# Bucket attention and a rational FFN on one core: token pieces loaded into the buffers of their parts, and operands, values and weights loaded at other steps

## The chip, the cores and the metric

The kernel runs on one core of a Trainium2 chip. A core has a matrix engine (TensorE, PE in the profile; its weight loads are PEld), a vector engine (VectorE, DVE), a scalar engine (ScalarE, ACT), a general one (GpSimd, POOL) and SyncE (SP), whose queue issues nearly all DMA transfers here. The metric is device time in microseconds (us) of one execution; lower is better.

## The reference

Two stages. Attention over 4 batches x 8 heads, 768 positions, head size 64, where a query sees only the keys of its own hash bucket; then a feed-forward network (FFN) with a rational function, over 3072 tokens of 512 values.

```python
q_bits = (einsum('bhsd,dk->bhsk', q, proj) > 0);  k_bits likewise
mask = bucket(q_bits)[:, :, :, None] == bucket(k_bits)[:, :, None, :]
scores = where(mask, q @ k.T / 8, -1e9);  scores -= scores.max(-1)
attn = exp(scores);  attn /= attn.sum(-1) + 1e-9
x = (attn @ v) rearranged to 3072 x 512
h = x @ w_in                                   # 512 x 2048
g = (a0 + a1*h + a2*h**2 + a3*h**3) / (1 + |b0|*|h| + |b1|*h**2 + 1e-6)
out = g @ w_out                                # 2048 x 512
```

`w_in` and `w_out` arrive as 64-bit floats; everything else and the output have 32 bits.

## The kernel before

Matrix products are made exact enough by splitting an operand into a rounded high part and the low part that is left, so that a product takes several passes.

**Attention** goes over 16 pairs of heads. For a pair `p`: `load(p)` brings the raw operands q and k into one of two buffers of the tag "raw" (`qkf` in the profile); `high` (ACT) and `low` (DVE) split them, `high_move`, `second_low` and `second_high` move parts between halves of the partitions (SP: `q<-q`, `k<-k`, `q<-lo`, `k<-lo`); `bits`, `penalties` and `maskrows` write mask rows (`q<-mb`, `k<-mb`); `maxstep` finds row maxima (`m<-psm`), which `shift_turn` and `shift_rows` put in as a row (`q<-mt`). Then twelve steps of `scores` (`pss`), each followed by exponentials on ACT (`E<-pss`) and sums of them (`acc`); `load_v` brings the values, and `values` multiplies them in two blocks of six steps (`psv<-E,v`); `values_out` copies the result (`col`, `xo`) and `values_store` stores it to memory (`x_d<-xo`). `sums` and `sums_store` do the same for the denominators (`psu`, `sr`, `s_d`), and `recips` turns the denominators of a batch into reciprocals in memory (`r_d`).

**Weights.** Beside attention, `weights(i)` prepares both weight matrices in 32 portions. An even `i` loads a portion of w_in (`wr<-w_in`), an odd one of w_out (`wr<-w_out`); two buffers `wr` serve both. ACT and DVE convert the portion from 64 bits in several steps (`ws<-wr`, `wr<-wr`, `ws<-ws,wr`) and split it; w_in stays on chip as `wi_hi` and `wi_lo`, w_out is stored to `wo_d` and comes back in the FFN.

**FFN.** Six blocks of 512 tokens. `Tokens.load(t, c)` brings a block in three pieces: values from `x_d`, reciprocals from `r_d` spread over 64 partitions, a product of both on DVE, a rounding copy on ACT into the high part `xh`, a subtraction on DVE into the low part `xl`. The parts of an even block lie in the two "raw" buffers; the last piece lies in two small ones. Per block 16 steps: `Gemm1` (`psh`), the rational function on ACT and DVE, the second product (`pso`). The first block's pieces are loaded while attention ends.

**Order.** The order of all work up to the FFN is written out by hand: `at(p, s, f, ...)` puts a call at place 12p+s, `spread` puts the parts of a generator (each up to its `yield`) at several places, and the calls are issued by rising place. Each engine and SP's queue keep that order. The numbers stand in the tables `MID`, `FIRST` (pairs 0 and 1) and `LAST` (the end). Some that matter here:

- `load(p)` at 12(p-4) + `MID["load"]` for p > 3; `load_v(p)` at 12(p-1) + `MID["load_v"]` for p > 1;
- the parts of `weights(i)` at 12(i // 2) + `MID["weights"][i % 2]`, for i < 2 those of `FIRST`;
- the parts of piece c of the first block at 180 + `LAST["tokens"][c]`: load, product, copy, subtraction;
- `coefficients` loads the FFN's coefficients (`ab<-coef`) at 12 and reads them on ACT (`absb`) at 14.

A DMA that fills a buffer which is still in use waits on SP, and what stands behind it on SP waits too.

Of the kernel before, what the change touches and what calls it, by code (L numbers as in the profile page):

```python
# [7 lines left out]
F32 = mybir.dt.float32  # L8
# [5 lines left out]
ALU = mybir.AluOpType  # L14
# [4 lines left out]
P = 128  # L19
S = 768  # L20
# [10 lines left out]
NCC = DM // P  # L31
NFC = DFF // P
NTK = 512
# [8 lines left out]
    group=6, values=[0.66, 0.05], values_out=3.5, maxima=7.17,  # L42
    maxima_steps=[0, 1.15, 1.73, 2.64, 3.32, 5.08, 5.86, 6.98, 8.0, 8.84, 10.26, 11.37], sums=14.65, sums_store=17.37,
    high=[-0.41, 1.19], low=[1.06, 3.35], bits=2.81, penalties=4.05, high_move=1.9, maskrows=5.61, second_low=-2.2,
    second_high=2.69, load_v=10.99, shift_turn=8.61, shift_rows=8.82, load=9.0, recips=[20.0, 22.0, 23.0],
    weights=[[1.44, 4.0, 4.1, 5.09, 5.49, 7.11, 9.5, 9.75, 17.5], [8.05, 10, 10.65, 11.5, 12.38, 14.29, 16.34, 19.32, 21.22]],
    weights_last=[0.5, 0.8, 1.0, 1.2],
)

# [1 line left out]
    maxima1=4.62, rate1=0.45, maxima2=9.5, rate2=0.82, high=[3.25, 3.53], low=[6.0, 7.3], bits=7.15, penalties=7.25,  # L51
    high_move=4.53, maskrows=8.2, second_low=4.25, second_high=4.35, load_v=4.78, group=2,
    values=[2.35, 2.65, 2.32, 2.35, 0.35, 0.61], values_out=3.02, high1=[-0.27, -5.58], low1=[11.24, 4.95],
    high_move1=20.05, load2=21.89, load3=3.8, penalties1=-6.57, maskrows1=3.69,
    weights=[[-5.7, 6.64, 6.7, 11.42, 12.19, 18.75, 21.75, 38.77, 44.13], [8.03, 9.04, 9.24, 11.12, 14.81, 15.27, 15.99, 17.91, 46.81]],
    warm=6, warms=[3, 3, 3, 1, 1, 1], maxima00=[-4.26, -2.29, -4.17, 1.67, -1.15, 2.77], shift00=[2.15, 4.99],
    shift0=[3.67, 3.44], ahead=3, scores=[[3.68, 3.82, 7.26], [6.03, 8.25, 12.4]], pen01=[4.77, 14.55], comp01=3.35,
# [3 lines left out]

LAST = dict(
    group=6, values=[0.28, 0.44], values_out=1.39, vout14=3.03,
    tokens=[[-7.43, -5.11, -2.83, -1.09], [-0.04, 3.83, 4.5, 5.2], [6.0, 9.38, 9.45, 9.53]], terms=7.05, ffn=[13.61, 16.09, 16.14],
    sums=16.96, wide=8, share=11, third=0, sums14=14.69, sumst14=22.46,
)
TINY = 2.0 ** -80
# [105 lines left out]
def attention(ctx, tc, nc, raw, ps_b, tail, tokens, early, operands_to_terms, ffn, load, QF, KF, v, w_in, w_out, wo_d, ident, cst, ones, prj,  # L173
# [302 lines left out]
    def at(p, s, f, *args):  # L476
        plan.setdefault(12 * p + s, []).append((f, args))
# [5 lines left out]
    for p in range(NPAIR):  # L483
        mid = 0 < p < NPAIR - 1
        n = MID["group"] if mid else (FIRST if p == 0 else LAST)["group"]
        for s in range(12):
            if p > 0 or s >= FIRST["ahead"]:
                at(p, s, scores, p, s)

            if p > 1:  # L490
                at(p - 2, MID["maxima"] + MID["maxima_steps"][s] if p > 2 else FIRST["maxima2"] + FIRST["rate2"] * s, maxstep, p, s)
            if s % n == n - 1:
                for i in range(s - n + 1, s + 1):
                    at(p, s + (MID["values"][s // n] if mid else (FIRST if p == 0 else LAST)["values"][s // n]), values, p, i)
            if s % NT == NT - 1:
                at(p, s + (LAST["vout14"] if (p, s) == (NPAIR - 2, 11) else MID["values_out"] if mid else (FIRST if p == 0 else LAST)["values_out"]), values_out, p, s // NT)
        for hf in range(2):
            at(p, 6 * hf + 9, values_store, p, hf)
        if p < NPAIR - 1:
            at(p, MID["sums"] if p < NPAIR - 2 else LAST["sums14"], sums, p)  # L500
            at(p, MID["sums_store"] if p < NPAIR - 2 else LAST["sumst14"], sums_store, p)
        if p > 1:
            for t in range(2):
                at(p - 2, (MID if p > 2 else FIRST)["high"][t], high, p, t)
                at(p - 2, (MID if p > 2 else FIRST)["low"][t], low, p, t, nc.vector if p > 2 else nc.gpsimd)
            if p % 2 == 0:
                at(p - 2, (MID if p > 2 else FIRST)["bits"], bits, p)
                at(p - 2, (MID if p > 2 else FIRST)["penalties"], penalties, p)
            at(p - 2, (MID if p > 2 else FIRST)["high_move"], high_move, p)
            at(p - 2, (MID if p > 2 else FIRST)["maskrows"], maskrows, p)  # L510
        if p > 0:
            at(p - 1, (MID if p > 1 else FIRST)["second_low"], second_low, p)
            at(p - 1, (MID if p > 1 else FIRST)["second_high"], second_high, p)
            at(p - 1, (MID if p > 1 else FIRST)["load_v"], load_v, p)
        if p > 1:
            at(p - 1, MID["shift_turn"], shift_turn, p)
            at(p - 1, MID["shift_rows"], shift_rows, p)
        if p > 3:
            at(p - 4, MID["load"], load, p)
        if p % NHP == NHP - 1 and p + 1 < NPAIR:  # L520
            spread(p, MID["recips"], recips(p // NHP))
    for i in range(2 * NFC):
        o = 12 * (i // 2)
        w = list(FIRST["weights"][i]) if i < 2 else list(MID["weights"][i % 2])
# [92 lines left out]
class Tokens:  # L617
# [214 lines left out]
```

## Time and profile before

| | before |
|---|---|
| median of 3 runs | 937.54 us (936.46 to 938.1) |
| the profiled execution, time | 937.44 us |
| its span, first to last instruction | 935.6 us |
| mean granted TensorE clock | 0.997 |
| busy share: PE, DVE, ACT, POOL | 99%, 90%, 69%, 47% |
| chain that ended last, by engine | PE 91%, DVE 3%, DMA 3%, ACT 2% |
| DMA moved | 111.57 MB, mean 119 GB/s |

The page gives busy times, a picture of the span in 40 slices, DMA queues, the chain of work that ended last, and the costliest groups of instructions. Attention with the weights takes the first 406 us or so, and the FFN the rest. In both, PE is busy nearly always. A row of the timeline has the start and the duration in us, the engine, the operation with its output and inputs, and in square brackets how long the engine was idle before it and what released it. SPq is the queue on which SP issues DMAs; the duration there is that of the issue, not of the transfer. All helper calls share line 93, so work is told apart by its tiles.

### The profile page before, as it was taken

The page shows a single profiled execution, that of the slowest core. Times are in us where ns is not written, and L with a number is a line of the kernel's source. Part 1 is how long each engine was busy: PE and PEld are TensorE (multiplying, and loading weights), DVE is VectorE, ACT ScalarE, POOL GpSimd, SP SyncE. Part 2 cuts the span into 40 slices and gives each one's busy share as a digit, 9 for nine tenths or more (in the row PEclk, how much of TensorE's full clock was granted, in tenths as well). Part 3 has the DMA queues.
Part 4 walks back from the last instruction along what each step waited for, and adds up shares of the span by engine and source line. Part 5 has one row for each costly group of instructions (what it writes and reads, how often), then busy time and mean ns, then how long its engine had stood idle before and what let it go on. Part 6 is the DMA issues. An engine that isn't in the chain of part 4 may idle for free.

```text
span 935.6 us, 13659 instructions
## 1 busy us (share of the span) xinstructions
PE 922.6 (99%) x4678; PEld 701.4 (75%) x4678; DVE 840.5 (90%) x1029; ACT 648.5 (69%) x1229; POOL 436.6 (47%) x362
## 2 busy tenths in 40 slices
PE   8999999999999999899999999999999999999997
PEld 4666666666767677568888888888888888888886
DVE  6799889878988898688998999899999999998996
ACT  7577767667767676777767776776676677677664
POOL 5587878777878787522222223223222222222222
PEclk9999999999999999999999999999999999999999
DMA  6768878778877778346412100210021002001001
GB/s 196 214 179 225 231 219 230 220 208 226 240 217 224 226 195 216 132 133 226 143 28 75 38 23 1 79 35 23 1 80 41 17 34 79 23 1 46 0 1 46
DMA packets 51243, 111.57 MB, mean 119 GB/s; under 512 B 9347, under 2 KB 20215, under 8 KB 51173
## 3 DMA queue, kind: packets, MB, share of 16 engines
q1 hardware_dynamic: 50740, 110.47, 40.3%
q8 instruction: 37, 0.61, 0.3%
q14 instruction: 34, 0.27, 0.1%
q10 hardware_dynamic: 432, 0.23, 0.1%
HBM read 56.82 MB, written 21.17 MB: 83 GB/s over the span
## 4 chain that ended last, share of the span: by engine, by line
PE 91%; DVE 3%; DMA 3%; ACT 2%; SPq 1%; issue 1%; ACTq 0%; DVEq 0%
PE psh L93 28%; PE pso L93 28%; PE pss L93 13%; PE psv L93 12%; PE psm L93 7%; PE psu L93 2%; DMA wr<-w_in 2%; DVE m L93 2%; PE psb L93 1%; SPq L93 1%; ACT E L93 1%; DMA r<-r_d 0%; DMA qkf<-kT 0%; DVE ws L93 0%; DVE wr L93 0%
## 5 line engine op out<-in xcount | busy, mean ns | idle before, releaser
L93 POOL TENSOR_TENSOR gl<-c,gh 128x512 fp32r<-128x512 f32 x96 | 134.6, 1402 | 387.6 <-ACT gh L93 378.3
L93 ACT ACTIVATE E<-pss 128x384 f32<-128x384 f32 x384 | 167.8, 493 | 106.1 <-PE pss L93 92.1
L93 PE MATMUL pso<-wo,gh 128*128 128x512 f32 x768 | 235.4, 389 | 0.0
L93 DVE TENSOR_REDUCE m<-psm 128x1 f32<-128x768 f32 x192 | 179.7, 949 | 34.7 <-PE psm L93 31.2
L93 POOL TENSOR_TENSOR acc<-E,E 128x384 f32<-128x384 f32 x124 | 154.4, 1263 | 87.7 <-ACT E L93 87.5
L93 PE MATMUL pss<-q,k 128*128 128x384 f32 (+2 forms) x768 | 171.9, 349 | 0.4 <-ACT col L93 0.4
L93 PEld LDWEIGHTS pso<-wo,gh 128*128 128x128 f32 x768 | 144.1, 188 | 29.8
L93 PEld LDWEIGHTS pss<-q,k 128*128 128x128 f32 (+2 forms) x768 | 136.2, 191 | 28.4 <-issue 17.0
L93 PE MATMUL psh<-xh,wi_hi 128*128 128x512 f32 x384 | 149.6, 390 | 0.0
L93 PE MATMUL psh<-xl,wi_hi 128*128 128x512 f32 x384 | 149.4, 389 | 0.0
L93 PE MATMUL psh<-xh,wi_lo 128*128 128x512 f32 x384 | 149.4, 389 | 0.0
L93 PE MATMUL pso<-wo,gl 128*128 128x512 f32 x384 | 148.4, 389 | 0.0
L93 ACT ACTIVATE h<-psh 128x512 f32<-128x512 f32 x96 | 57.4, 598 | 130.7 <-PE psh L93 130.6
L93 POOL TENSOR_TENSOR acc<-acc,E 128x384 f32<-128x384 f32 x123 | 137.3, 1135 | 11.1 <-ACT E L93 10.9
L93 PE MATMUL psv<-E,v 128*64 128x385 f32 x768 | 134.3, 492 | 4.0 <-ACT E L93 3.5
L93 DVE SCALAR_TENSOR_TENSOR c<-c,ab,r 128x512 f32<-128x512 f32 x96 | 135.6, 1413 | 0.0
L93 PEld LDWEIGHTS psv<-E,v 128*64 128x64 f32 x768 | 52.6, 136 | 71.4 <-issue 61.8
L93 PE MATMUL psm<-k,q 76*128 76x384 f32 (+1 forms) x384 | 102.2, 348 | 1.8 <-DVE m L93 1.0
L93 DVE SCALAR_TENSOR_TENSOR w<-h,absb,w 128x512 f32<-128x512 f32 x96 | 74.0, 771 | 15.4 <-ACT w L93 15.2
L93 PEld LDWEIGHTS psh<-xh,wi_hi 128*128 128x128 f32 x384 | 72.0, 187 | 16.1 <-issue 1.2
L93 PEld LDWEIGHTS pso<-wo,gl 128*128 128x128 f32 x384 | 72.1, 188 | 15.1
L93 PEld LDWEIGHTS psh<-xl,wi_hi 128*128 128x128 f32 x384 | 72.1, 188 | 14.9
(78 smaller groups left out, 1218.3 us busy)
## 6 DMA issues: line engine op xcount, KB each, us to landing
q<-q SPq DMA_DIRECT2D x45, 192.0 KB
k<-k SPq DMA_DIRECT2D x45, 192.0 KB
wr<-w_in SPq DMA_DIRECT2D x16, 512.0 KB
wr<-w_out SPq DMA_DIRECT2D x16, 512.0 KB
wo_d<-wr SPq DMA_DIRECT2D x16, 512.0 KB
wo<-wo_d SPq DMA_DIRECT2D x16, 512.0 KB
qkf<-qT SPq DMA_DIRECT2D x16, 384.0 KB
qkf<-kT SPq DMA_DIRECT2D x16, 384.0 KB
```

What stands on the lines that cost most here:

```text
L93: return self.tc.keep_in_program_order(issue(*args, **kwargs))
```

## The change

Two things. First, `Tokens.load` no longer loads values and reciprocals into the buffers "lo0" and "lo1": it loads the values into the place of the low part and the reciprocals into the place of the high part, multiplies both into a new tile `y` ("lo0" for pieces 0 and 2, "lo1" for piece 1), rounds `y` into the high part and subtracts into the low part. The number of instructions and of bytes stays the same. The parts' tiles are taken when the load is issued, not after the product.

Second, places in the order change: raw operands from 9.0 to 5.7 (pair 4 keeps 9.0), values from 10.99 to 8.9, the load of each w_in portion but the first from 1.44 to -1.0, and most parts of the token pieces.

```diff
-    second_high=2.69, load_v=10.99, shift_turn=8.61, shift_rows=8.82, load=9.0, recips=[20.0, 22.0, 23.0],
-    weights=[[1.44, 4.0, 4.1, 5.09, 5.49, 7.11, 9.5, 9.75, 17.5], [8.05, ...]],
+    second_high=2.69, load_v=8.9, shift_turn=8.61, shift_rows=8.82, load=5.7, recips=[20.0, 22.0, 23.0],
+    weights=[[-1.0, 4.0, 4.1, 5.09, 5.49, 7.11, 9.5, 9.75, 17.5], [8.05, ...]],
...
-    high_move1=20.05, load2=21.89, load3=3.8, penalties1=-6.57, maskrows1=3.69,
+    high_move1=20.05, load2=21.89, load3=3.8, load4=9.0, penalties1=-6.57, maskrows1=3.69,
...
-    tokens=[[-7.43, -5.11, -2.83, -1.09], [-0.04, 3.83, 4.5, 5.2], [6.0, 9.38, 9.45, 9.53]], terms=7.05, ...
+    tokens=[[-8.9, -5.11, -2.83, -1.09], [-2.9, 1.5, 2.2, 3.83], [7.1, 10.4, 10.5, 10.6]], terms=7.05, ...
...
-            at(p - 4, MID["load"], load, p)
+            at(p - 4, MID["load"] if p > 4 else FIRST["load4"], load, p)
...
     def load(self, t, c):
-        nc, raw = self.nc, self.raw
-        w = min(S, NCC * NTK - c * S)
-        x = raw.tile([P, w], F32, tag="lo0", name=f"x{t}_{c}", bufs=1)
-        r = raw.tile([P, w], F32, tag="lo1", name=f"r{t}_{c}", bufs=1)
+        nc = self.nc
+        hi, lo = self.place(t, c, "h"), self.place(t, c, "l")
+        w = hi.shape[1]
+        x, r = lo.bitcast(F32), hi.bitcast(F32)
...
         yield
-        nc.vector.tensor_tensor(out=x, in0=x, in1=r, op=ALU.mult)
-        yield
-        hi, lo = self.place(t, c, "h"), self.place(t, c, "l")
-        nc.scalar.copy(hi, x)
-        yield
-        nc.vector.tensor_tensor(out=lo, in0=x, in1=hi.bitcast(F32), op=ALU.subtract)
+        y = self.raw.tile([P, w], F32, tag=f"lo{c % 2}", name=f"y{t}_{c}", bufs=1)
+        nc.vector.tensor_tensor(out=y, in0=x, in1=r, op=ALU.mult)
+        yield
+        nc.scalar.copy(hi, y)
+        yield
+        nc.vector.tensor_tensor(out=lo, in0=y, in1=hi.bitcast(F32), op=ALU.subtract)
```

More of the change, by code (lines that the diff above doesn't have):

```diff
@@ L44 @@
     high=[-0.41, 1.19], low=[1.06, 3.35], bits=2.81, penalties=4.05, high_move=1.9, maskrows=5.61, second_low=-2.2,
-    second_high=2.69, load_v=10.99, shift_turn=8.61, shift_rows=8.82, load=9.0, recips=[20.0, 22.0, 23.0],
-    weights=[[1.44, 4.0, 4.1, 5.09, 5.49, 7.11, 9.5, 9.75, 17.5], [8.05, 10, 10.65, 11.5, 12.38, 14.29, 16.34, 19.32, 21.22]],
+    second_high=2.69, load_v=8.9, shift_turn=8.61, shift_rows=8.82, load=5.7, recips=[20.0, 22.0, 23.0],
+    weights=[[-1.0, 4.0, 4.1, 5.09, 5.49, 7.11, 9.5, 9.75, 17.5], [8.05, 10, 10.65, 11.5, 12.38, 14.29, 16.34, 19.32, 21.22]],
     weights_last=[0.5, 0.8, 1.0, 1.2],
@@ L63 @@
     group=6, values=[0.28, 0.44], values_out=1.39, vout14=3.03,
-    tokens=[[-7.43, -5.11, -2.83, -1.09], [-0.04, 3.83, 4.5, 5.2], [6.0, 9.38, 9.45, 9.53]], terms=7.05, ffn=[13.61, 16.09, 16.14],
+    tokens=[[-8.9, -5.11, -2.83, -1.09], [-2.9, 1.5, 2.2, 3.83], [7.1, 10.4, 10.5, 10.6]], terms=7.05, ffn=[13.61, 16.09, 16.14],
     sums=16.96, wide=8, share=11, third=0, sums14=14.69, sumst14=22.46,
```

## The prediction, made before the changed kernel ran

> **What bounds the kernel now.** I read the head of the page first: the span, and how much of it TensorE (PE) works.
>
> ```profile
> span 935.6 us, 13659 instructions
> ...
> PE 922.6 (99%) x4678; PEld 701.4 (75%) x4678; DVE 840.5 (90%) x1029; ACT 648.5 (69%) x1229; POOL 436.6 (47%) x362
> ```
>
> PE is idle for 935.6 - 922.6 = 13.0 us in all, and apart from a lowered clock that is all that a change of loads can win. The run that was profiled took 937.44 us, 1.84 us more than its span, and the median of the runs shown is 937.54 us; I reckon against 937.44. About 0.2% of it, 1.9 us, is what a measurement of this kernel can tell from no change.
>
> Next the timeline around the passage from the last attention pair (15) to the FFN, where the page's slices show PE below full share. I write "step 12p+s" for a place in the written plan: step s of pair p.
>
> ```profile
> 376.36 0.37 SPq L93 DMA_DIRECT2D v<-v  x1
> ...
> 381.59 0.32 SPq L93 DMA_DIRECT2D x<-x_d  x1
> ...
> 384.45 0.58 ACT L93 ACTIVATE xo<-psv,col 128x384 f32<-128x384 f32 x1
> ...
> 384.79 1.36 DVE L93 TENSOR_TENSOR acc<-E,E 128x384 f32<-128x384 f32 x1
> 384.90 0.58 SPq L93 DMA_DIRECT2D wr<-w_in  x1
> ...
> 389.23 0.96 DVE L93 TENSOR_TENSOR x<-x,r 128x768 f32<-128x768 f32 x1 [2.41 <-DMA r<-r_d]
> ...
> 390.20 0.67 ACT L93 ACTIVATE ws<-wr 128x512 f32<-128x512 f32 x1 [2.74 <-DMA wr<-w_in]
> ...
> 392.61 1.24 PE L93 MATMUL psv<-E,v 128*64 128x385 f32 x4 [2.15 <-ACT E L93]
> ...
> 395.66 0.32 SPq L93 DMA_DIRECT2D x<-x_d  x1
> ...
> 401.76 0.62 ACT L93 CAST xh<-x 128x512 fp32r<-128x512 f32 x1 [2.45 <-DVE x L93]
> ...
> 404.70 1.25 PE L93 MATMUL psv<-E,v 128*64 128x385 f32 x4 [0.63 <-ACT E L93]
> ...
> 405.87 0.50 PE L93 MATMUL psh<-xh,wi_hi 128*128 128x512 f32 x1
> ```
>
> Read it by releasers. ScalarE (ACT) stands still 2.74 us before 390.20 for `wr<-w_in`; the last exponential of the first half of pair 15 is queued behind that, and PE waits 2.15 us for it before 392.61. ACT stands still again 2.45 us before 401.76, for the third token piece's product on VectorE (DVE), whose load was issued at 395.66. FFN products start at 405.87. The waits of the SP queue and of the engines say why the two loads were late:
>
> ```profile
> SPq L93 <- DVE xl L93: 133.2, 12, 17.0
> ```
>
> ```profile
> ACT ws L93 <- DMA wr<-w_in: 7.3, 4, 3.5
> ```
>
> SP held token pieces until `xl` of the piece before was written, because both pieces used the same two buffers; the weight load stood behind the second piece (381.59, then 384.90). The wait for `wr<-w_in` came four times, 7.3 us in total, so there is one more large one. The chain shows what it cost:
>
> ```profile
> 129.66 4.03 PE psv L93 x24
> ...
> 177.28 4.03 PE psv L93 x24
> ...
> 226.38 4.03 PE psv L93 x24
> ```
>
> ```profile
> 192.26 0.59 SPq L93 DMA_DIRECT2D v<-v  x1
> 192.89 0.49 SPq L93 DMA_DIRECT2D wr<-w_in  x1
> ```
>
> ```profile
> 203.07 0.69 ACT L93 ACTIVATE ws<-wr 128x512 f32<-128x512 f32 x1 [3.50 <-DMA wr<-w_in]
> ```
>
> Value blocks of the same place lie two pairs apart: 177.28 - 129.66 = 47.62 us, then 226.38 - 177.28 = 49.10. The second is 1.5 us too long, and it holds the 3.50 us ACT wait for the load issued at 192.89, with the values issued just before at 192.26.
>
> **The change part by part.** *Token pieces (t = 0).* The number of instructions stays; only a buffer `y` for the product is new, alternating between two, and nothing in SP's order waits for `xl` any more. Piece 2 moves from step 179.96 to 177.10, ahead of the first weight load of the next group, which moves from 181.44 to 179.00. SP is free after the values' load (376.36), so piece 2 goes out at about 376.8. In the old run the same six issues took 384.90 - 381.59 = 3.3 us, so `wr<-w_in` goes out at about 380.1, 4.8 us earlier, and its 2.74 us wait goes. What is late next: the product of piece 2 now stands at step 181.5 on DVE and its rounding copy at 182.2 on ACT, directly behind the copy `xo`, which ends at 384.45 + 0.58 = 385.03. DVE is busy with the sum `acc` until 384.79 + 1.36 = 386.15, and the product takes 0.96 (row 389.23), so ACT now waits from 385.03 to 387.11, 2.1 us, ahead of three exponentials. Net gain there: 2.74 - 2.08 = 0.66 us.
>
> *Piece 3* moves from step 186.0 to 187.10 but loses its wait. SP can issue it once the store of `xo` has gone (about 385.6, estimated from 385.03) instead of at 395.66, so the data are there some 10 us earlier. Its ACT copy now stands at 190.5, behind the exponential of step 190, not ahead of it, so the 2.45 us wait no longer holds that. But the last load of w_out (step 188.05) and its conversion now stand ahead of the copy, and the product still follows DVE's sums. I let half of the 2.45 us come back as those waits and take 1.2 us; the ends are 0 and 2.45. The passage then gives 0.66 + 1.2 = 1.9 us, and psh starts near 404.0.
>
> *The clock.* The same passage was also slow in another way:
>
> ```profile
> 394.00:395.00 1.00, 1.00 (x5) 1.00 (x5) 1.00 (x3) 0.49 (x1) 0.00 (x0) 0.65 0.05 16
> 395.00:396.00 1.00, 1.00 (x5) 1.00 (x4) 1.00 (x2) 0.91 (x3) 0.00 (x0) 0.50 0.00 0
> 396.00:397.00 1.00, 1.00 (x4) 1.00 (x4) 0.19 (x1) 0.81 (x3) 0.03 (x1) 0.50 0.36 49
> 397.00:398.00 1.00, 1.00 (x5) 1.00 (x5) 0.70 (x1) 1.00 (x3) 0.98 (x1) 0.64 0.86 291
> ```
>
> The granted clock in the last column but two was 0.65, 0.50, 0.50 and 0.64 in four slices of 1 us, 1.7 us lost, right after the 2.15 us gap. My new gap is about 0.7 us shorter. [...] I credit nothing here: ACT, not PE, set most of that stretch. The ends are 0 and 1.7 us of gain.
>
> *Raw operands, values, weights in the middle pairs.* In each pair SP's order was: mask rows, `wo_d` store, `w_out`, shift rows, `x_d` store, raw operands (2 x 384 KB), low parts (4 x 192 KB), values, `w_in`. It becomes: mask rows, raw operands, `wo_d`, `w_out`, shift rows, values, `x_d`, low parts, `w_in`. Values go out right after the shift rows, past seven transfers, and `w_in` has 0.79 MB less ahead of it. For a price of 0.79 MB I take this row:
>
> ```profile
> 120.00:144.00 24.00, 24.00 (x153) 16.64 (x153) 21.22 (x25) 17.13 (x38) 18.85 (x17) 1.00 0.78 218
> ```
>
> 218 GB/s at a DMA share of 0.78 is 279 GB/s when busy, so 0.79 MB takes 2.8 us. The stall of 3.50 us thus shrinks to below 1 us, and of its 1.5 us I take 1.2 as won. In the other middle pairs PE is busy 24.00 of 24 us, as here, so an earlier load wins nothing.
>
> What this pays for is `w_out`, which now stands behind the raw operands in 11 pairs (1 to 11):
>
> ```profile
> 109.73 0.45 SPq L93 DMA_DIRECT2D wo_d<-wr  x1
> ...
> 115.65 0.67 ACT L93 ACTIVATE ws<-wr 128x512 f32<-128x512 f32 x1
> ...
> 116.14 4.10 PE L93 MATMUL psv<-E,v 128*64 128x385 f32 x24
> ...
> 116.78 0.87 ACT L93 ACTIVATE E<-pss 128x384 f32<-128x384 f32 x2
> ```
>
> ```profile
> 207.74 0.45 SPq L93 DMA_DIRECT2D wo_d<-wr  x1
> ```
>
> ```profile
> 212.74 0.68 ACT L93 ACTIVATE ws<-wr 128x512 f32<-128x512 f32 x1 [0.33 <-DMA wr<-w_out]
> ```
>
> The raw operands go out where `wo_d` did, so `w_out` lands 2.8 us later. In the worst pair it was there 212.74 - 207.74 = 5.0 us after `wo_d` was issued (ACT waited 0.33); in the usual pair ACT comes for it 115.65 - 109.73 = 5.92 us after. With the same landing ACT now waits 5.0 + 2.8 - 5.92 = 1.9 us in a usual pair. Behind it stands the exponential of step 11: its first half ends at 116.78 + 0.87 / 2 = 117.2, and PE reads it after 20 of 24 value products, at 116.14 + 4.10 x 20 / 24 = 119.6. So 2.3 us are free, and 1.9 are covered. Where ACT comes early, as at 212.74, the wait is 2.8 us and 0.5 are lost; that pair was early only because of the stall before it. I take 0.2 us lost; the ends are 0 and 5.5 us (0.5 in each of 11). The shift rows also stand behind this: the queue ahead of them is done 5.0 + 2.8 = 7.8 us after `wo_d` used to be issued, and the scores that need them follow the value block, which ends at 116.14 + 4.10 = 120.2, 10.5 us after it: covered.
>
> *First pair.* `w_in` number 2 moves from 13.44 to 11.00, ahead of the coefficients at 12.00, but its buffer comes free only where it did, since it uses that of number 0.
>
> ```profile
> 48.53 0.59 SPq L93 DMA_DIRECT2D ab<-coef  x1
> 50.47 0.33 SPq L93 DMA_DIRECT2D wr<-w_in  x1
> ```
>
> ```profile
> 52.08 0.22 ACT L93 ACTIVATE absb<-ab 128x1 f32<-128x1 f32 x1
> ...
> 53.58 0.48 ACT L93 COPY sr<-psu 128x384 f32<-128x384 f32 x1 [0.61 <-PE psu L93]
> ...
> 54.88 0.62 ACT L93 CAST wr<-ws 128x512 fp32r<-128x512 f32 x1
> ```
>
> ```profile
> 56.51 1.50 DVE L93 TENSOR_TENSOR wr<-ws,wr 128x512 fp32r<-128x512 f32 x1
> ```
>
> ```profile
> 384.90 5.28 DMA wr<-w_in
> ```
>
> So the coefficients go out after 50.47 instead of at 48.53, behind 512 KB. The only row with the time of such a load is the last, 5.28 us with token pieces ahead of it; with an emptier queue I estimate 4.1, so 54.6 at the earliest and 55.8 with 5.28. ACT comes for them at 52.08 and waits 2.5 us; 0.61 was idle anyway (row 53.58), so the cast of 54.88 ends near 57.4 instead of 55.50, and DVE's subtraction starts 0.9 us after its 56.51. DVE is on the chain here. I take +0.9; the ends are 0 (the small transfer passes the large one) and +2.1. [...]
>
> *The rest.* In the FFN only buffers change; PE runs without a gap, and token loads there lose a wait of SP that nobody waits for: 0.
>
> Sum: -1.9 (passage) - 1.2 (stall at 203) + 0.2 (`w_out`) + 0.9 (coefficients) = -2.0; 937.44 - 2.0 = 935.4 us.
>
> **The rivals.** *The passage only trades waits.* The product of piece 2 holds ACT as long as the weight load did, the last w_out load holds the last exponential, and the stall at 203 belongs to this one execution. For it: the new 2.1 us wait above, nearly the old 2.74. Against it: 2.45 us at 401.76 has no such heir. It gives 937.44 - 0.66 + 0.9 = 937.7; the same if the pieces still waited for something and nothing moved.
>
> *`w_out` becomes the late load.* Place: the conversion at step 10 of pairs 1 to 11. From a delay of 3.2 us on, instead of 2.8, ACT's wait passes the 2.3 us of cover in the usual pair too, and every further 0.1 us costs 1.1. At 3.7 us it is 11 x 0.5 = 5.5 in place of the 0.2 in the sum: 940.7. For it: old loads were waited for at 0.33 already, so they come just in time. Against it: 279 GB/s is a mean over mixed traffic, and the queue is nearly idle where the raw operands now go.
>
> **How the numbers follow.** Forecast, faster by over 0.2%: 0.47 (935.4; its own range 933.0 to 935.6). Waits traded, within 0.2%: 0.37 (937.7, and forecasts that fall short by a little). `w_out` late: 0.16 (940.7). For 8 in 10 the range goes down to 933.0 (passage 0.66 + 2.45 = 3.1, stall 1.2, nothing lost for `w_out` and coefficients: 933.1) and up to 939.0, which leaves out about 0.1 at each end.
>
> **What would show it.** Right: second token piece and `w_in` issued near 377 and 380, no ACT wait on `w_in` near 390, a new one of about 2 us on DVE near 385; psh near 2 us earlier after the last middle pair; no wait for `w_in` above 1 us near 203; an ACT wait of about 2 us for the coefficients near 52; waits of ACT for `w_out` in most of pairs 1 to 11, with PE still at 24.00 of 24. Wrong: PE below 23.8 in middle stretches (the `w_out` rival), or a passage as long as before from 376 to psh.

## The result, and the profile after

The changed kernel is slower: 942.19 us (median of 4 executions, 941.64 to 943.69) against 937.52 us (4 executions) for the kernel before. The ratio is 1.0054, 95% interval 1.0036 to 1.0071. The forecast was 935.4 us. The profiled execution took 941.64 us, 4.20 us more than that of before. The head of its page:

```profile
span 939.8 us, 13716 instructions
...
PE 925.0 (98%) x4678; PEld 700.4 (75%) x4678; DVE 834.2 (89%) x1029; ACT 647.6 (69%) x1229; POOL 434.0 (46%) x362
```

PE's busy time grew by 2.4 us (from 922.6), its idle time by 1.8 (939.8 - 925.0 = 14.8 against 13.0). More than half of the loss thus does not look like idleness in this view; the reason follows below. The profiled execution is the fastest of the four and has a mean granted clock of 0.998; the other three have 0.994 or 0.995, so some 3 us more of PE's work went to a lowered clock in them (0.0035 x 940), at places that no profile shows, though they took only 0.5 to 2.1 us longer. What follows accounts for the profiled one.

To see where the time went, compare when the same work starts. The table has the start of blocks of 24 value products (`psv`), two to a pair, and of the first FFN product (`psh`), from the timelines of PE. "Before" is a time, the others are differences to it, all in us.

```
place                     before  after   e1     e2     e3     e6     e8     e11
pair 1, first block        57.04  +1.95  +3.69  -0.27  +0.70  -0.15  -0.36  +4.45
pair 1, last block         68.67  +1.91  +4.74  -0.24  +0.69  -0.14  -0.36  +5.24
pair 2, first block        82.17  +2.49  +4.73  +7.62  +0.68  -0.15  -0.36  +5.23
pair 5, last block        163.68  +2.43  +5.39  +8.51  +0.65  +0.38  -0.37  +5.17
pair 6, first block       177.21  +3.23  +5.38  +9.17  +0.62  +0.50  -0.36  +5.14
pair 7, last block        212.80  +1.70  +4.27  +7.56  -1.02  -1.12  -1.99  +4.66
pair 8, last block        237.16  +2.18  +4.93  +7.54  -1.06  -0.84  -2.00  +4.65
pair 9, first block       249.41  +3.84  +4.90  +8.83  -1.06  +3.83  -1.61  +4.64
pair 13, last block       355.10  +6.04  +6.54 +10.67  -0.45  +4.49  -1.63  +5.87
pair 15, first block      387.00  +6.05  +6.55 +10.67  -0.43  +4.50  -1.62  +5.87
pair 15, last block       399.75  +4.61  +5.08  +9.21  -1.90  +3.09  -2.77  +4.92
first psh                 405.87  +4.04  +4.49  +8.62  -2.49  +2.50  -3.92  +5.86
```

The column "after" has four parts: +1.9 up to pair 1; +5.1 in seven steps behind pairs 1, 5, 7, 8, 9, 10 and 11 (0.58, 0.80, 0.46, 1.66, 0.70, 0.25, 0.62); -1.5 where the kernel before stood still near 203; and -2.0 from pair 15 to psh. A last +0.6 at pair 13 comes with a subtraction `lo<-qkf,k` on DVE that took 1.83 us instead of 0.94; e10, e11 and e14 show the same step there, with the loads of the middle pairs where the kernel before has them, so it is not the change's. Together 1.9 + 5.1 - 1.5 - 2.0 + 0.6 = +4.1.

The passage to the FFN gained what was forecast. Timeline of after:

```profile
382.65 0.42 SPq L93 DMA_DIRECT2D xl<-x_d  x1
...
386.85 0.59 SPq L93 DMA_DIRECT2D wr<-w_in  x1
...
391.53 0.38 SPq L93 DMA_DIRECT2D xl<-x_d  x1
...
393.09 0.83 ACT L93 CAST xh<-y 128x768 fp32r<-128x768 f32 x1 [2.01 <-DVE y L93]
...
397.94 1.24 PE L93 MATMUL psv<-E,v 128*64 128x385 f32 x4 [0.66 <-ACT E L93]
...
407.12 0.62 ACT L93 CAST xh<-y 128x512 fp32r<-128x512 f32 x1 [1.29 <-DVE y L93]
...
408.74 1.24 PE L93 MATMUL psv<-E,v 128*64 128x385 f32 x4 [0.93 <-ACT E L93]
...
409.91 0.50 PE L93 MATMUL psh<-xh,wi_hi 128*128 128x512 f32 x1
```

The second piece goes out as soon as SP is there, `wr<-w_in` comes in time, and ACT has no wait for it. The copy of piece 2 waits 2.01 us for DVE (forecast 2.1), PE then 0.66 us instead of 2.15. From pair 15's first block to psh it takes 409.91 - 393.05 = 16.86 us, against 405.87 - 387.00 = 18.87.

The waits of after say what took its place:

```profile
ACT ws L93 <- DMA wr<-w_out: 23.7, 13, 3.2
...
ACT xh L93 <- DVE y L93: 4.3, 3, 2.0
...
ACT absb L93 <- DMA ab<-coef: 3.4, 1, 3.4
```

The columns are sum, count and longest. ACT's waits for `wr<-w_out` were 1.3 us in all before; they are 23.7 now. The wait for the coefficients is new, and those for `wr<-w_in`, 7.3 us before, are gone.

### The profile page after: what moved, and what is told of

Its sections match the earlier page's. It is cut to its first block, busy times and chain, and to the rows that moved or that the text cites. A ratio compares the mean times of both kernels' runs of the same rounds, so it can differ in the third digit from the quotient of the medians.

```text
span 939.8 us, 13716 instructions
## 1 busy us (share of the span) xinstructions
PE 925.0 (98%) x4678; PEld 700.4 (75%) x4678; DVE 834.2 (89%) x1029; ACT 647.6 (69%) x1229; POOL 434.0 (46%) x362
## 4 chain that ended last, share of the span: by engine, by line
PE 87%; DVE 6%; DMA 3%; ACT 2%; issue 1%; SPq 0%; ACTq 0%; DVEq 0%
PE psh L93 28%; PE pso L93 28%; PE pss L93 11%; PE psv L93 11%; PE psm L93 6%; DVE m L93 3%; DMA wr<-w_out 2%; PE psu L93 2%; PE psb L93 1%; DVE ws L93 1%; ACT E L93 1%; DVE wr L93 1%; DMA ab<-coef 0%; PE psw L93 0%; ACT wr L93 0%
## 5 line engine op out<-in xcount | busy, mean ns | idle before, releaser
L93 POOL TENSOR_TENSOR gl<-c,gh 128x512 fp32r<-128x512 f32 x96 | 137.1, 1428 | 385.1 <-ACT gh L93 375.7
L93 PEld LDWEIGHTS pss<-q,k 128*128 128x128 f32 (+2 forms) x768 | 134.3, 189 | 32.5 <-issue 17.7
L93 POOL TENSOR_TENSOR acc<-acc,E 128x384 f32<-128x384 f32 x123 | 131.4, 1087 | 22.7 <-ACT E L93 22.6
L93 PE MATMUL psv<-E,v 128*64 128x385 f32 x768 | 137.7, 493 | 3.1 <-ACT E L93 2.9
L93 DVE SCALAR_TENSOR_TENSOR c<-c,ab,r 128x512 f32<-128x512 f32 x96 | 138.7, 1445 | 0.0
```

The lines of the kernel that those rows point to most:

```text
L93: return self.tc.keep_in_program_order(issue(*args, **kwargs))
```

## The experiments

All kernels of one comparison ran on the same chip with the kernel before, whose median there was 937.0 (e1 to e4), 936.96 (e5 to e8), 937.37 (e9 to e12) and 937.87 us (e13 to e15).

```
run                                             time us, median (range, n)       ratio to before, 95%
after  the change                               942.19 (941.64 to 943.69, 4)     1.0054 [1.0036, 1.0071]
e1  after, raw operands back at 9.0             945.77 (941.91 to 950.03, 6)     1.0098 [1.0072, 1.0124]
e2  after, coefficients first again             943.92 (942.05 to 947.01, 6)     1.0078 [1.0060, 1.0095]
e3  before, token pieces alone                  934.95 (933.49 to 937.62, 12)    0.9979 [0.9969, 0.9988]
e4  before, raw operands at 5.7 alone           947.44 (946.49 to 948.97, 4)     1.0117 [1.0103, 1.0132]
e5  after, both back                            938.96 (936.52 to 944.84, 12)    1.0027 [1.0011, 1.0042]
e6  e2, early operands only from pair 6 on      937.46 (936.69 to 939.96, 11)    1.0004 [0.9995, 1.0013]
e7  e2, operands right behind w_out             934.86 (933.99 to 935.64, 7)     0.9976 [0.9965, 0.9987]
e8  e6, conversion behind the exponentials      933.92 (933.14 to 934.37, 5)     0.9965 [0.9954, 0.9977]
e9  e6, denominators loaded later               937.55 (935.86 to 941.22, 12)    0.9997 [0.9979, 1.0014]
e10 e3, conversion behind the exponentials      934.90 (933.43 to 936.82, 12)    0.9972 [0.9957, 0.9986]
e11 before, coefficients late alone             942.24 (937.10 to 943.40, 12)    1.0039 [1.0022, 1.0055]
e12 e7, conversion behind the exponentials      934.69 (934.07 to 935.67, 12)    0.9965 [0.9952, 0.9978]
e13 after, conversion behind the exponentials   939.13 (935.88 to 940.30, 12)    0.9995 [0.9980, 1.0011]
e14 e11, PE's gap filled                        940.57 (937.49 to 944.83, 12)    1.0030 [1.0014, 1.0045]
e15 e5, values back as well                     934.99 (934.53 to 936.67, 10)    0.9969 [0.9957, 0.9981]
```

**e1 and e2: take back one of the two faults.**

```diff
-    ... shift_rows=8.82, load=5.7, ...
+    ... shift_rows=8.82, load=9.0, ...              # e1 (and e5)
...
         w = list(FIRST["weights"][i]) if i < 2 else list(MID["weights"][i % 2])
+        if i == 2:
+            w[0] = 1.44                             # e2 (and e5 to e9, e12, e15)
```

> The changed kernel with only the raw operands' load put back from 5.7 to 9.0, behind the w_out load again; token pieces, values and w_in stay as changed. Theory W (late w_out: the 512 KB of w_out stand behind 768 KB of raw operands, ACT waits 1.2 to 3.2 us for them in eleven pairs, and PE loses what exceeds about 1.6 us): the ACT waits for w_out go below 0.5 us, the 3.5 to 4 us that the value blocks lose between pairs 2 and 13 go, and the time is about 942.2 - 4 = 938.2 us. Rival T (the values and w_in, moved as well, or the token tiles, cost the time in the middle pairs): the middle pairs keep most of the loss, 941 to 942 us.

> The changed kernel with only the second w_in portion's load (i = 2) put back to 1.44, so that the coefficients go out ahead of it in pair 1; all else as changed. Theory C (the small coefficient load stands behind a 512 KB load that itself waits for its buffer; ACT waits 3.4 us for it and PE loses 1.9 us in the first pairs): ACT's wait for the coefficients falls below 0.5 us, the value block that started at 70.58 starts near 68.7, and the time is about 942.2 - 1.9 = 940.3 us. Rival (the first pair's loss is made up by a stall that comes later, since the next w_out load is late anyway): 941.5 to 942.2 us.

Both expectations failed: e1 is slower than the full change, by intervals that just part, and e2, whose interval overlaps with it, is not faster. In e1 the w_out waits did go, but the column still rises by 2.9 us between pairs 2 and 10, against 1.1 won at the stall; PE waits for DVE there, 1.27 us at the longest, and e5 below shows the reason. The first pairs lost 4.7 us instead of 2.5, with nearly the same wait for the coefficients (3.20 us against 3.38). This execution, 941.91 us, is the fastest of e1's six; what made the others slower, up to 950.03 us at mean clocks from 0.991 to 0.995, is in no profile. PE's gap and the stretch behind it, first in after, then in e1 (timeline of PE, and stretches, where the granted clock is the last column but two):

```profile
56.62 1.01 PE L93 MATMUL pss<-q,k 77*128 77x384 f32 x4 [2.15 <-ACT sr L93]
```

```profile
56.00:60.00 4.00, 3.38 (x18) 2.51 (x20) 2.45 (x5) 4.00 (x10) 1.68 (x2) 1.00 0.93 201
```

```profile
56.59 1.65 PE L93 MATMUL pss<-q,k 77*128 77x384 f32 x4 [1.97 <-ACT sr L93]
```

```profile
56.00:57.00 1.00, 0.41 (x1) 0.41 (x2) 0.48 (x1) 1.00 (x4) 0.00 (x0) 0.58 0.99 212
57.00:58.00 1.00, 1.00 (x4) 1.00 (x4) 0.15 (x1) 1.00 (x3) 0.00 (x0) 0.50 1.00 203
...
62.00:63.00 1.00, 1.00 (x6) 0.47 (x4) 0.86 (x2) 0.00 (x0) 1.00 (x1) 0.51 0.23 54
```

After nearly the same gap (2.15 us and 1.97) the clock stayed at 1.00 in the profiled execution of after and fell to half in e1. A slice at half clock throughout shows 0.50, so twice what it lacks of 1.00 is its time at half clock: 0.84 and 0.98 us in the outer two, 1 in each of the five between, together 6.82 us. That is 3.4 us of work lost, and PE reads as busy in nearly all of it (1.00 of each slice from 57 on): one reason why its busy time is 925.4 us in e1, against 922.6 in the kernel before.

In e2 the coefficients were in time, and ACT came to pair 1's conversion 2.2 us earlier (68.04 instead of 70.20), but had `w_out` no earlier, at 72.75 (after: 72.30). The wait grew from 2.10 to 4.71 us (e2: a row of ACT, the row of PE that follows from it, and stretches of 1 us):

```profile
72.75 0.66 ACT L93 ACTIVATE ws<-wr 128x512 f32<-128x512 f32 x1 [4.71 <-DMA wr<-w_out]
```

```profile
74.42 1.24 PE L93 MATMUL psv<-E,v 128*64 128x385 f32 x4 [2.54 <-ACT E L93]
```

```profile
75.00:76.00 1.00, 1.00 (x4) 0.41 (x2) 0.00 (x0) 0.47 (x1) 1.00 (x2) 0.81 0.95 296
...
84.00:85.00 1.00, 1.00 (x12) 0.34 (x8) 0.00 (x0) 0.44 (x1) 0.00 (x0) 0.50 1.02 215
85.00:86.00 1.00, 1.00 (x12) 0.24 (x8) 0.00 (x0) 0.04 (x1) 0.00 (x0) 0.57 0.97 177
```

Gap 2.54 us, then half clock for 0.38 + 9 + 0.86 = 10.24 us: 7.9 us lost where after lost 0.58 for `w_out`. So in the full change the coefficients' wait hid most of pair 1's wait for w_out, and e2, which takes back the first alone, exposes the second. The half clock belongs to some executions: two of e2's six have a mean clock of 0.999 and took 942.05 and 942.46 us, no more than the full change.

**e3 and e4: one part alone.** e3 has the rewritten `Tokens.load` and its places; e4 has the operands' load at 5.7 (pair 4 at 9.0).

> The kernel before with only the token pieces changed: the new loads into the places of the parts, the tile y, and the new places of the pieces; raw operands, values and w_in stay where they were. Theory (the passage from the last pair to the FFN gains by the pieces alone): the first FFN product comes 1.2 to 2.0 us earlier, 935.5 to 936.3 us. Rival (the gain of the passage needs the earlier values and w_in: w_in portion of the last pair still goes out behind the second piece's place or the values): the wait of ACT for w_in at about 390 stays and the time is 936.5 to 937.5 us. The stall at 203 of the kernel before is not touched and should be there again, 1.5 us, if it belongs to the order and not to one execution.

> The kernel before with only the raw operands' load moved from 9.0 to 5.7 (pair 4 keeps 9.0), as the change has it. Theory W: w_out is late by itself, ACT waits for it 1 to 3 us in most of pairs 1 to 11, PE loses 3.5 to 4.5 us in the middle pairs, the stall at 203 (1.5 us) goes since w_in no longer stands behind the raw operands: 937.5 + 4 - 1.5 = 940 us, range 939 to 941.5. Rival T (late w_out is covered and the time was lost by values and w_in): 936 to 938 us.

e3: 934.95 us; psh comes 2.06 us earlier than pair 15's block does (-0.43 to -2.49), as in the full change. The gain belongs to the pieces alone. The stall at 203 is not there in e3, nor in e10, with all loads of the middle pairs where they were before. With the same loads it is there in e11: ACT waits 3.02 us for `wr<-w_in` before 207.74, and the block takes 5.22 us instead of 4.10. In e14 ACT waits 2.06 us before 181.19 and the block takes 5.07. So the stall does not come in every execution, but in three of the five profiled with that order. e4 is slower than either theory said: a wait of 5.00 us for w_out in pair 1, a gap of 2.83 us, and half clock for 10.24 us, as in e2. The middle pairs lost some 2 us more, which the missing stall at 203 nearly makes up. At the passage to the FFN, which e4 leaves as it was, a second half clock follows (e4: a row of PE, and the first and last slice):

```profile
401.61 1.24 PE L93 MATMUL psv<-E,v 128*64 128x385 f32 x4 [2.42 <-ACT E L93]
```

```profile
402.00:403.00 1.00, 1.00 (x5) 0.40 (x4) 1.00 (x1) 0.00 (x0) 0.69 (x1) 0.88 1.03 426
...
409.00:410.00 1.00, 1.00 (x6) 1.00 (x5) 0.15 (x1) 0.00 (x0) 0.00 (x0) 0.71 0.88 350
```

It lasts 0.24 + 6 + 0.58 = 6.82 us and costs little: the way from pair 15 to psh is 0.5 us longer than in the kernel before, which has 3.42 us of half clock on it. PE waits for ACT there (2.42 us in the row above), which I take as the reason why a slower PE loses little.

**e5 and e15: both back, then the values too.** e5 joins the edits of e1 and e2; e15 has besides `load_v=10.99`.

> The changed kernel with both taken back: the raw operands' load at 9.0, and the w_in portion i = 2 at 1.44 behind the coefficients. Token pieces, values (8.9) and the other w_in loads stay as changed. The run with only the raw operands put back kept the coefficient wait (ACT 3.20 us at 55.31, PE gap 1.97 us) and there the granted clock was 0.50 for some 6.5 us behind it; the run with only i = 2 put back had no coefficient wait but an ACT wait of 4.71 us for w_out in pair 1, a PE gap of 2.54 us and the clock at 0.50 for some 10 us. Theory (two faults, each of which makes a gap that the clock answers; values and w_in early cost nothing): neither gap is there, no stretch at half clock before 400 us, 934.5 to 935.5 us, like the kernel with the token pieces alone (934.95). Rival (the earlier values or w_in cost time themselves, in the first pairs or by contention with w_out): 937 us or more.

> The changed kernel with the raw operands at 9.0, i = 2 of w_in at 1.44, and the values back at 10.99 as well; what is left of the change is the token pieces and the earlier w_in (from i = 4 on). The same with values at 8.9 gave 938.96 us, with gaps of 0.4 to 0.6 us behind DVE waits for the low parts' moves. Theory V (values and raw operands ahead of the low parts' moves make those late, DVE waits for the buffers): those DVE waits go, 934.5 to 935.5 us. Rival I (the earlier w_in stands in the way): 937 us or more.

e5 has neither gap and no half clock near 72, yet takes 938.96 us. What is new in its list of waits is DVE's, for a buffer that moves of low parts still read; and in PE's timeline a gap behind it, one of several:

```profile
DVE lo L93 <- DMA q<-lo: 5.6, 6, 1.8
```

```profile
199.79 0.62 PE L93 MATMUL psm<-k,q 76*128 76x384 f32 x2 [0.63 <-DVE m L93]
```

With operands at 9.0 and values at 8.9 both stand ahead of the four moves `q<-lo`, `k<-lo`, and these are late. With the values back (e15) these waits fall from 5.6 to 0.3 us and the time is 934.99 us; theory V holds in the time. The earlier values cost about 4 us by the medians (938.96 to 934.99) and more by the ratios. The traces show 2.7 us of it between pairs 1 and 15, where e5 loses 1.9 us and e15 gains 0.7, so the DVE waits as the only cause are not shown. With the operands at 5.7 or 8.1, ahead of the values, there is no such loss: e7 has no such DVE wait and e8 one of 0.3 us, at 934.86 and 933.92 us (below). The earlier w_in costs nothing and wins nothing that can be told from e3 (e15 934.99 us, e3 934.95). e1 has operands and values in the order of e5, and the same kind of DVE wait (3.0 us in five waits): besides the coefficients' wait it carries this fault, which the full change does not have.

**e6 to e8: w_out in pairs 2 to 11.** e6 keeps the early operands from pair 6 on, e7 loads them right behind w_out, e8 is e6 with the conversion later.

```diff
-            at(p - 4, MID["load"] if p > 4 else FIRST["load4"], load, p)
+            at(p - 4, MID["load"] if p > 5 else FIRST["load4"], load, p)      # e6, e8, e9
...
-    ... load=5.7, ...
+    ... load=8.1, ...                                                         # e7, e12
...
-    ... [8.05, 10, 10.65, 11.5, 12.38, ...
+    ... [8.05, 11.1, 11.2, 11.5, 12.38, ...                                   # e8, e10, e12, e13
```

> The changed kernel with i = 2 of w_in at 1.44 (coefficients first), and the raw operands' load early (5.7) only from pair 6 on: pair 5's load, which is issued in pair 1, goes back to 9.0. So w_out stands behind raw operands in pairs 2 to 11 and not in pair 1. Theory (in pairs 2 to 11 ACT waits 1.2 to 3.2 us for w_out, and PE loses what exceeds about 1.6 us, with no half clock): no gap near 72, 3 to 4.5 us lost between pairs 2 and 12, 938 to 939.5 us. Rival H (ACT now comes 2 us earlier than in the changed kernel and the waits are longer; gaps above 2 us and a half clock appear in a middle pair as they did in pair 1): above 941 us. Rival N (pair 1 alone made the loss): 935 to 936 us.

> The changed kernel with i = 2 of w_in at 1.44, and the raw operands' load at 8.1 instead of 5.7, directly behind the w_out load (8.05) and ahead of the shift rows (8.82) and the values. Theory Q (what hurt w_out is only that 768 KB stood ahead of it in SP's queue, not that the operands load at the same time): no ACT wait for w_out above 0.5 us, shift rows 2.8 us later but covered: 934.5 to 935.5 us. Rival B (the transfers share bandwidth whatever their order of issue): ACT waits for w_out of 1 us or more remain and the time is 937 us or more. Rival S (the shift rows become late): PE waits ahead of the first scores of the pairs.

> As the run with the early raw operands from pair 6 on, and besides the two ACT steps of the w_out conversion moved from 10 and 10.65 to 11.1 and 11.2, behind the last exponentials of the pair instead of ahead of them. Theory (what PE loses to the late w_out goes through the exponential of step 11, which stands behind ACT's wait): ACT may still wait for w_out, but the values block has its exponential and PE loses under 1 us in pairs 2 to 12, 935 to 936 us. Rival (the late conversion itself is what matters, through DVE or the next steps of ACT): the loss stays or grows, 938 us or more.

e6 gives the scale of a wait. ACT's waits for w_out in pairs 4, 5, 7 and 11, and the value blocks in which they fall, from the chain (start, duration):

```profile
141.92 0.69 ACT L93 ACTIVATE ws<-wr 128x512 f32<-128x512 f32 x1 [1.33 <-DMA wr<-w_out]
...
165.35 0.69 ACT L93 ACTIVATE ws<-wr 128x512 f32<-128x512 f32 x1 [1.68 <-DMA wr<-w_out]
...
213.14 0.68 ACT L93 ACTIVATE ws<-wr 128x512 f32<-128x512 f32 x1 [1.83 <-DMA wr<-w_out]
...
313.23 0.70 ACT L93 ACTIVATE ws<-wr 128x512 f32<-128x512 f32 x1 [1.95 <-DMA wr<-w_out]
```

```profile
141.04 4.03 PE psv L93 x24
...
164.13 4.16 PE psv L93 x24
...
211.75 4.32 PE psv L93 x24
...
311.74 4.44 PE psv L93 x24
```

A wait of 1.33 us leaves the block at 4.03; 1.68, 1.83 and 1.95 make it 4.16, 4.32 and 4.44. From about 1.55 us on, each 0.1 us costs 0.1, and PE still counts as busy. In pair 8 the wait is 4.68 us (e6: rows of ACT and of PE, and the first and last slice of the half clock behind):

```profile
240.65 0.66 ACT L93 ACTIVATE ws<-wr 128x512 f32<-128x512 f32 x1 [4.68 <-DMA wr<-w_out]
```

```profile
242.31 1.24 PE L93 MATMUL psv<-E,v 128*64 128x385 f32 x4 [2.54 <-ACT E L93]
```

```profile
243.00:244.00 1.00, 1.00 (x5) 0.51 (x3) 0.00 (x0) 0.36 (x1) 1.00 (x2) 0.86 0.77 280
...
247.00:248.00 1.00, 1.00 (x7) 1.00 (x7) 0.76 (x2) 1.00 (x2) 1.00 (x1) 0.94 0.00 0
```

The loss there is 4.67 us (from -0.84 to +3.83): 2.54 of gap, some 1.7 of half clock (0.28 + 3 + 0.12 = 3.40 us of it), and the 0.4 left for the break in PE's run of products, of which more below. The other nine pairs lost some 1.7 us together. This execution took 939.96 us, the most of the eleven; the median of e6 is 937.46, between theory N and the first theory, at a mean clock of 0.999.

In e7 the operands go out just behind w_out instead of ahead, 2.4 steps later, and the waits nearly go; in e8 they stay but stand behind the last exponentials (the waits of e7, then of e8):

```profile
ACT ws L93 <- DMA wr<-w_out: 3.9, 3, 1.8
```

```profile
ACT ws L93 <- DMA wr<-w_out: 9.7, 11, 2.5
```

e7 takes 934.86 us, as theory Q had it, though waits above 0.5 us stay (1.32, 1.78 and 0.75 us in pairs 0, 1 and 8); e8 takes 933.92, a little less than its theory asked. What hurt was mainly the order in SP's queue, and the way from the wait to PE goes through the exponential of step 11. e10 and e12 put the same conversion on e3 and on e7:

> The kernel before with the token pieces changed (934.95 us by itself) and the two ACT steps of the w_out conversion at 11.1 and 11.2; raw operands, values and w_in at their old places. Theory (what the late conversion wins beyond hiding late loads is the gap of 0.9 us in the last pair, where it no longer stands ahead of the last exponential): 933.9 us, as with the early loads. Rival (the late conversion only wins where w_out is late): 934.9 us.

> The changed kernel with i = 2 of w_in at 1.44, the raw operands at 8.1 behind the w_out load (934.86 us by itself), and the w_out conversion's ACT steps at 11.1 and 11.2. Theory (both remedies together give no more than the late conversion alone, since by then no load is on PE's path): 933.5 to 934.2 us. Rival (the late conversion pushes ACT's work into the next pair's scores when nothing was late): 935 us or more.

934.90 and 934.69 us: where w_out is in time the late conversion gives nothing that can be told apart; the rival of e10 holds, and e12 lies between its theory and its rival. e8 and e12 have the lowest ratio, 0.9965, and beat both kernels; their intervals overlap with those of e3, e7, e10 and e15.

**e9: why pair 8?** The load of the denominators (`rs<-s_d`) stands just ahead of w_out there; e9 has `recips=[21.0, 24.0, 25.0]`.

> As the run with the early raw operands from pair 6 on (937.46 us; one gap, 2.54 us before 242.31 in pair 8, behind an ACT wait of 4.68 us for w_out), and besides the load of the reciprocals' denominators moved from step 20 to 21 behind the w_out load, with its arithmetic at 24 and its store at 25. Denominators are loaded in pairs 4, 8 and 12, just ahead of w_out. Theory R (in pair 8 that load of 24 KB in small pieces makes w_out later still): the wait in pair 8 falls to about 2 us like its neighbours', the gap and the half clock behind it go, 934.5 to 935.5 us. Rival (pair 4 has that load too and waits only 1.33 us, so pair 8 is late for something else): the gap stays, 937 to 938 us.

The row of ACT in pair 8:

```profile
238.93 0.68 ACT L93 ACTIVATE ws<-wr 128x512 f32<-128x512 f32 x1 [2.94 <-DMA wr<-w_out]
```

The wait fell from 4.68 to 2.94 us, without half clock, but the waits of pairs 2 to 11 besides are 1.2 to 2.6 us, and the median did not move. Inconclusive: ACT gets w_out 7.6 to 8.2 us after its issue in pair 8 (after, e6, e9), where 6.4 is usual, and why stays open.

**e11, e13 and e14: the coefficients by themselves, and the clock.** e11 is the kernel before with `spread(1, (1.5, 2), coefficients())`; e13 is after with the late conversion, so that the coefficients' wait is left; e14 is e11 with products in the gap:

```diff
+    def fill(n):
+        ps = ps_a.tile([P, 2, 512], F32, tag="psa", name="psf")
+        for _ in range(n):
+            nc.tensor.matmul(ps[:, 0, 0:256], prj_b, cst_b, start=True, stop=True)
...
+    at(0, 15.99, fill, 24)
```

> The kernel before with only the coefficients' load moved from 12 to 13.5, just behind the w_in load at 13.44; ACT reads them at 14 as before. Theory (the coefficients' delay costs by itself, as seen in the changed kernel: ACT waits about 3.4 us, PE has a gap of about 2 us): 937 + 2 = 939 us, and 3 us more in executions where the clock answers the gap, so a wide spread from 938.5 to 943. Rival (as predicted at first, +0.9 or nothing): 937 to 938 us.

> The changed kernel with only the two ACT steps of the w_out conversion moved to 11.1 and 11.2; raw operands, values, w_in and the coefficients' place stay as changed. Theory (the coefficients' wait by itself makes the larger part of the loss): the gap of about 2 us near 55 stays, with half clock behind it in most executions; the middle pairs lose nothing: 933.9 + 2 to 5 = 936 to 939 us, wide spread. Rival (w_out was nearly all of it, and the first pair's loss is absorbed later): 934 to 935 us.

> The kernel before with the coefficients' load at 13.5 (942.24 us by itself; PE gap 3.36 us before 58.40, granted clock 0.50 from about 59.9 to 63.8), and 24 products of 128 x 256 bf16 of a constant, which nobody reads, placed on PE right ahead of the stalled scores (15.99): some 2.6 us of work in the gap. Theory G (PE's idleness lowers the clock): ACT still waits over 4 us for the coefficients, the gap is split into pieces under 1.6 us, no stretch at half clock follows, and 2 us or more of the loss go: 939 to 940.3 us, narrow spread. Rival (the clock drops for something else, such as the burst of work after the stall): half clock stays, 942 us or more.

e11 loses 4.9 us by this one place in the medians, 3.7 by the ratio (rows of ACT and PE, and slices of the half clock):

```profile
57.11 0.20 ACT L93 ACTIVATE absb<-ab 128x1 f32<-128x1 f32 x1 [4.59 <-DMA ab<-coef]
```

```profile
58.40 1.02 PE L93 MATMUL pss<-q,k 77*128 77x384 f32 x4 [3.36 <-ACT sr L93]
```

```profile
59.00:60.00 1.00, 1.00 (x7) 1.00 (x6) 0.34 (x1) 1.00 (x4) 0.00 (x0) 0.89 1.03 183
...
63.00:64.00 1.00, 1.00 (x10) 0.36 (x8) 0.86 (x2) 0.00 (x0) 1.00 (x2) 0.90 0.19 45
```

The wait is 4.59 us, the gap 3.36, the half clock 0.22 + 3 + 0.20 = 3.42 us. In e14 the gap is full of unread products, 24 in 2.79 us, and the clock stays at 1.00 (a row of PE, one of ACT, and two stretches of 4 us):

```profile
54.88 2.79 PE L93 MATMUL psf<-cst 128*128 128x256 bf16 x24
```

```profile
55.94 0.20 ACT L93 ACTIVATE absb<-ab 128x1 f32<-128x1 f32 x1 [3.41 <-DMA ab<-coef]
```

```profile
56.00:60.00 4.00, 4.00 (x30) 3.50 (x29) 2.42 (x5) 3.97 (x11) 1.08 (x1) 1.00 0.99 206
60.00:64.00 4.00, 4.00 (x25) 1.68 (x22) 3.11 (x5) 1.23 (x3) 3.97 (x4) 1.00 0.30 75
```

Pair 1's last block starts 2.63 us late there instead of 5.24. But the load was also quicker: ACT had it 4.75 us after its issue, against 6.22 in e11, and waited 3.41 us, not over 4 as expected. Without the products the gap would have been about 2.2 us, an estimate from the end of the copy `sr` at 57.17; and after, with a wait of 3.38 us and a gap of 2.15, kept its clock without them. The medians, 940.57 and 942.24 us from two comparisons, do not part the two kernels by their intervals either, and the spread of e14 was not narrow. So e14 does not decide whether PE's idleness brings the half clock; for it speaks that every half clock in attention stands behind a gap (of 1.97 to 3.36 us). In e13 the w_out losses are gone, and the time falls to 939.13 us, by 3.1 us in the medians and 5.5 by the ratios of the two comparisons. Its gap before 58.22 is 1.98 us. Behind 1.97 us the clock fell to 0.50 in e1; here it stayed at 1.00 in the profiled execution, one of five of the twelve that took 935.88 to 937.16 us at a mean clock of 0.999 or 1.000, and seven took 939.05 to 940.30 at 0.995 or 0.996. From e13 to e8, which has the coefficients first (and pair 5's load late), it is another 5.2 us in the medians and 2.8 by the ratios.

## Why the prediction was wrong

**Right.** The passage: -1.9 forecast, -2.0 measured, and e3 shows it as a part by itself. The waits named went, but the split was luck: 0.66 and 1.2 forecast for the two pieces, 1.4 and 0.6 measured in the table's columns (from +6.05 to +4.61 at the last block of pair 15, then to +4.04). Nothing was credited for the clock there, which was right: e11, with the old passage and no half clock on it, takes as long for it as the kernel before. The FFN: unchanged, 0.16 us between psh and the end.

**Right in size, in part by luck.** The stall at 203: -1.2 forecast, -1.5 in the two traces. ACT's waits for `wr<-w_in` do go with the moved loads: after has none, nor have e6, e7 and e8. But e3 and e10 do not lose the time either, and no load of the middle pairs was moved in them. The rival "the passage only trades waits" was half right: a stall of some executions was counted in full.

**Wrong, the largest: `w_out`, +0.2 forecast, +5.1 measured.** The wait itself was well placed: 1.9 us forecast in the usual pair, and the eleven waits in after average 21.9 / 11 = 1.99. Two steps failed. First, the cover. I took PE's need of the exponential at 20/24 of a block and found 2.3 us free; the rows of PE and ACT in pair 5 of after show what is missing:

```profile
166.11 3.45 PE L93 MATMUL psv<-E,v 128*64 128x385 f32 x20
169.80 1.24 PE L93 MATMUL psv<-E,v 128*64 128x385 f32 x4 [0.24 <-ACT E L93]
```

```profile
168.12 0.68 ACT L93 ACTIVATE ws<-wr 128x512 f32<-128x512 f32 x1 [2.39 <-DMA wr<-w_out]
```

In a run the last four products take 4.10 - 3.45 = 0.65 us; when they have to wait they take 1.24. That break costs 0.59 us, so the free cover is not 2.3 but about 1.6, and a wait of 2.39 lost 0.80 (0.24 of it shown as idle). Second, the spread. I priced a usual pair; the waits go from 1.18 to 3.21, and with a threshold in their midst the mean says little. My rival "`w_out` becomes the late load" named the mechanism, but asked for a delay of 3.2 us and had 0.16. Its sign, PE below 23.8 of 24 us in a middle stretch, came in two of eleven stretches of after (23.76 from 168 to 192, 22.95 from 240 to 264); the losses in the others count as busy.

**Wrong: the coefficients, +0.9 forecast, +1.9 in after, about 4 to 5 alone.** The landing at 54.6 and a wait of 2.5 were estimated, from a load time of 4.1 us that no row gave; these are the rows of after, of SP and of ACT:

```profile
50.23 0.34 SPq L93 DMA_DIRECT2D wr<-w_in  x1
50.62 0.42 SPq L93 DMA_DIRECT2D ab<-coef  x1
```

```profile
55.34 0.20 ACT L93 ACTIVATE absb<-ab 128x1 f32<-128x1 f32 x1 [3.38 <-DMA ab<-coef]
...
56.10 0.47 ACT L93 COPY sr<-psu 128x384 f32<-128x384 f32 x1
```

ACT had the load at 55.34, 4.72 us after its issue behind the 512 KB of `wr<-w_in`, and waited 3.38. I then followed the delay into the cast and DVE's subtraction, and not into what else stands behind `absb` on ACT: the copy `sr<-psu`, which frees the buffer that the next scores write, and the exponentials. PE stopped for `ACT sr`, 2.15 us. In this term and in that of `w_out` I assumed that a load waits for what SP issued ahead of it. The 4.72 us for a load of 128 x 6 values agrees, though a share of the bandwidth with the large load could give the same, and no run here parts the two; for `w_out`, e7 speaks for the order (waits of 3.9 us in all against 23.7).

**Missing: a price for the gap itself.** No term of the sum, and no end of a range, held a new half clock as a loss, though the profile of before showed one behind a gap of 2.15 us and the prediction quoted it. Gaps of 2.0 to 2.5 us cost 1.9 us in after, 4.7 in e1 and e6 and 7.9 in e2, and in the profiled executions of e1, e2 and e4 much of the loss is this. It did not make the miss of the profiled execution of after, which has no half clock before its end and took 941.64 us all the same: there the two terms above did. The upper end of 939.0 was too low for them already: it does not reach the 940.7 of the prediction's own `w_out` rival.

## What to carry to other kernels

Price a load that moves ahead of another by what stands behind the waiting instruction on its engine, all of it up to the buffers it frees, and by the spread of the waits over all repetitions, not by a usual one. The cover ends earlier than the place of the products in the block says: here by 0.6 us, since four products that had to wait took 1.24 us, and 0.65 in a run. From gaps of about 2 us on (1.97 us was the shortest here with a half clock behind it, 2.20 the longest without), add 1.7 us, half of the 3.41 below, or a multiple as a chance, where PE sets the pace: where it did not, in e4, 3.40 us more of half clock cost 0.5. When a change moves several loads, undo more than one part at a time too: here the coefficients' wait hid most of pair 1's wait for w_out, and the operands' way back brought out a fault of the earlier values.

## What the runs showed of the hardware

The half clock came in whole pieces. Its lengths in the profiled executions, that at the very end left out, were 3.42 (before, 394.3 to 397.7), 3.40 (e6), 3.42 (e11), 6.82 (e1), 10.24 (e2), and 10.24 and 6.82 us (e4): one, two or three times 3.41. In the profiles of all seventeen kernels, the five gaps of PE of 2.42 us or more were followed by it (e2 2.54, e4 2.83 and 2.42, e6 2.54, e11 3.36), of the six from 1.94 to 2.20 two (before 2.15, e1 1.97) and not the others (after 2.15, e11 1.94, e13 1.98, e14 2.20), of those up to 1.55 none. It began 1.54 us after the start of the gap in e1, 3.95 in e6 and 4.74 in e11. So the length of a gap alone does not tell whether it follows, nor when: 1.97 us was enough in e1, and 2.20 us was not in e14. Why it lasted three pieces in e2 and e4, with PE busy again, stays open.
